# Pairwise flips of K and Q, and an own unit order for each segment of a group, in a two-branch attention kernel

## The chip, the cores and the metric

The kernel runs on one core of a Trainium2 chip. The metric is device time in microseconds (us) from the start to the end of one execution; a smaller one is better. A profiled execution gives the trace that all durations below come from.

The engines carry the names of the profile: PE multiplies matrices (PEld is its loading of the stationary operand), DVE is the vector engine, ACT the scalar engine (exponentials, logarithms, copies with a scale), POOL the general one, SP issues the DMAs. PE writes to PSUM, eight banks of 128 partitions by 512 fp32 words; DVE and ACT read PSUM and copy to SBUF.

## What is computed

A gate `g = sigmoid((x * gate_w).sum(-1))` mixes two branches on the same `x` (2048 tokens, 512 wide): `g * a + (1 - g) * b`.

Branch A is recurrent, segment by segment, 32 heads of 128:

```python
mem = mem0                                   # 8 rows
for s in range(64):                          # segments of 32 tokens
    h = concatenate([mem, x[32*s : 32*s+32]])     # 40 rows
    q, k, v = h @ Wq, h @ Wk, h @ Wv              # per head
    p = softmax(where(mask, q @ k.T * scale, -1e9))   # 40 x 40 for each head
    o = (p @ v) over all heads @ Wo               # 40 x 512
    mem = o[:8]                              # what the next segment starts from
    outs.append(o[8:])
```

Branch B is causal attention of 32 heads of 16 in four blocks of 512 tokens, with a memory of the earlier blocks (`M += phi(k).T @ v`, `z += sum phi(k)`), mixed by `sigmoid(beta)` and followed by `@ wo`. Its blocks do not wait for each other's attention.

All data are bf16; sums are fp32 in PSUM.

## The kernel before

Each engine gets a list of operations in the order in which the Python code records them (`Prog.op`). An operation waits by semaphore for the last writer of what it reads and the last readers of what it writes. PSUM banks are handed out when an operation is recorded (`Banks.take`, `pair`, `give`): an operation that gets a bank waits until the copy out of it has been made that last used it. So the order of recording sets both each engine's queue and which bank follows which.

First come the loads, the transpose of x and B's projections (to about 81 us of the trace). Then `plan_a` goes through the 64 segments of A, four to a group. Of a segment's 40 rows, 32 go through PE together: the 8 rows of memory and 24 tokens. The last 8 tokens of each of four segments ("left" rows) form a block of 32 rows that is projected a group ahead (`left_units`, L875), and their output projection and fold come a group later (`ol_units`, L938).

Within a segment the work is cut into units, and `A_ORDER` (L828) lists in which order they are recorded, the same list for every segment. b is 0 or 1, one for each half of the heads:

- `Q0x Q0y`, and so with K and V: the projection of half the heads, each in two halves of the contraction (x: channels that need the first half of the new memory, y: the second). `proj`, matmuls at L867.
- `k0 q0 v0`: the copy of such a projection out of PSUM, L320 on ACT or L322 on DVE, as `A_ENG` says (L832).
- `TK0 TQ0`: the flip. Four 32-row blocks of heads lie side by side over the partitions, and a 32 x 32 block transpose on DVE (`flip`, L872) makes them 128 x 32 per head.
- `S0`: scores, mask first (L1054), then 16 heads (L1057) and the left keys (L1061). `X0` exponential on ACT (L1070), `M0` row sums by a matmul with ones (L1087), `L0` logarithm and exponential for the reciprocal on ACT (L1094, L1097), `N0` the normalising multiply on DVE (L1101), `n0` its left part on POOL (L1107).
- `PV0`: values times probabilities (L1117) and at once its left part (L1126), into two pairs of banks; `E0a E0b` copy them out.
- `W0a` ... `W1b`: output projection (L908). `H0 l0`: its bf16 high half (copy on ACT, L915) and low half (subtraction on DVE, L920); `F0 F1` fold four partial sums into the new memory and rows (L930), `hm0 hm1` copy the memory to the next segment's input (L1163), `ax` copies the other rows (L1169).

Between these stand units of other work that PE can do meanwhile. `bS` takes one of B's 160 score blocks (matmuls at L711, and, in the same unit, the exponential on ACT at L719 and the causal mask on POOL at L727), if fewer than two are ahead of their PV; `bP` does the PV of a block (L758); `bT` does what follows every fifth one: a chain of seven small DVE operations (L791 to L807) behind a matmul bN (L786), or a transpose (L818). `Fc` and `Ff` take the next filler: the left projections with their copy and flip, the left rows' output projection with its high and low halves, its fold, or a group's final mixing (L991, L1006). B's blocks are spread over the first 57 segments (`nseg_b`, L851).

Of the kernel before, what the change touches and what calls it, by code (L numbers as in the profile page):

```python
# [223 lines left out]
def build(nc, es, A_x, A_mem0, A_Wq, A_Wk, A_Wv, A_Wo, B_wq, B_wk, B_wv, B_wo, B_beta, gate_w, out, dbg=None):  # L224
    v = NS()
# [30 lines left out]
    def alloc(stack, *specs):  # L256
        for name, shape, dt, n in specs:
# [24 lines left out]
    alloc(esA, ("LN_sb", [128, 2, 512], BF16, 0), ("KTL", [128, H, SEG], BF16, 2), ("QTL", [128, H, SEG], BF16, 2),  # L282
          ("VL", [128, 2, 512], BF16, 2), ("xL", [128, C, SEG], BF16, 2), ("KN_sb", [128, 2, 512], BF16, 0), ("QN_sb", [128, 2, 512], BF16, 0),
          ("KT_sb", [128, H, SEG], BF16, 0), ("QT_sb", [128, H, L], BF16, 0), ("V_sb", [128, 2, 512], BF16, 0),
# [84 lines left out]
def plan_const(v):  # L369
# [14 lines left out]
    sel(ident[:], [[-1, 128]], ALU.not_equal, 1.0, 0, 1, ri, "ident1")  # L384
    rz = Rs("KTz")
# [257 lines left out]
class BAttn:  # L643
# [3 lines left out]
    def __init__(self, v):  # L647
        self.v = v
        self.n = 0
        self.late = []  # L650
        self.total = 16 * 2 * 5
        self.pv_n = 0
        self.blocks = {}
        self.loaded = set()
        self.obk = None
        self.jobs_done = 0
# [27 lines left out]
    def scores(self):  # L684
# [30 lines left out]
        if k == 4:  # L715
            self.load(job + 1, G, "k")
        pt = v.PT[n % 2]
# [110 lines left out]
A_ORDER = """  # L828
    Q1x Q1y K0x K0y Q0x Q0y k0 K1x K1y V0x q0 q1 V0y k1 TK0 TQ0 v0 S0 TQ1 bP X0 bS V1x TK1 V1y M0 L0 v1
    S1 N0 X1 Fc M1 L1 n0 n1 PV0 E0a E0b N1 Fc bP PV1 W0a E1b W0b E1a bT W1b W1a H0 H1 bP l0 l1 bS  # L830
    Ff F0 F1 hm0 hm1 Ff bS ax Ff""".split()
A_ENG = dict(K0="act", K1="act", Q0="act", Q1="dve", V0="act", V1="dve", KL0="act", KL1="act", QL0="act", QL1="act", VL0="act", VL1="act", OL="act", ax="dve", hm="dve", n="gp", E0a="dve", E0b="act", E1a="act", E1b="act", last=0)  # L832


def plan_a(v, nseg):
# [14 lines left out]
    ORDER, ENG = DEV.get("order") or A_ORDER, DEV.get("eng") or A_ENG  # L850
    n_b0, nseg_b = bat.n, DEV.get("nseg_b", 57)  # L851
    last_half = 0 if ORDER.index("E1a") > ORDER.index("E1b") else 1
# [19 lines left out]
    def flip(dst, src, reads, writes, name):  # L872
        P.op("dve", lambda d: d.transpose(dst, src), reads=reads, writes=writes, name=name)  # L873

    def left_units(g):  # L875
# [7 lines left out]
        for m, w_sb, wr, nat in (("K", Wk_sb, "Wk", LN_sb), ("Q", Wq_sb, "Wq", LN_sb), ("V", Wv_sb, "Wv", VL[par])):  # L883
            rn = ["LN%d" % b if m != "V" else "VL%d_%d" % (par, b) for b in range(2)]
            for b in range(2):
                def u(m=m, w_sb=w_sb, wr=wr, nat=nat, b=b, rn=rn):
                    bk = B.take()
                    proj(bk, lhs, w_sb, b, m != "V", [Rs("xL%d" % par), Rs(wr)], "%sL%d_%d" % (m, g, b))
                    evac(ENG["%sL%d" % (m, b)], nat[:, b, :], pb[bk], [bk], [Rs(rn[b])], "%sLev%d_%d" % (m, g, b))
                    B.give(bk)  # L890
                    if m != "V":
                        dst = (KTL if m == "K" else QTL)[par]
                        flip(dst[:, 16 * b:16 * (b + 1), :], nat[:, b, :].rearrange("p (n e) -> p n e", e=SEG), [Rs(rn[b])],
                             [Rs("%sTL%d_%d" % (m, par, b))], "%sLt%d_%d" % (m, g, b))
                units.append(("c", u))
# [17 lines left out]
    def part_hi(bks, hf, hi, res, name):  # L913
        c = slice(HD * hf, HD * (hf + 1))
        P.op("act", lambda a: a.activation(hi[:, c], pb[bks[hf]][:, 0:HD], ACT.Copy), reads=[rbank[bks[hf]]],  # L915
             writes=[Rs(res[0][hf])], name="%sh%d" % (name, hf))
# [21 lines left out]
    def ol_units(g):  # L938
# [5 lines left out]
        for b in range(2):  # L944
            def u(b=b):
# [4 lines left out]
                if b == 1:  # L950
                    for hf in range(2):
                        part_hi(st["bks"], hf, LN_sb[:, 0, :], o_res, "olev%d" % g)
                        part_lo(st["bks"], hf, LN_sb[:, 0, :], LN_sb[:, 1, :], o_res, "olev%d" % g)
            units.append(("c", u))

        def ut():
            bks = B.pair()
            for hf in range(2):
                fold(bks, hf, LN_sb[:, 0, :], LN_sb[:, 1, :], o_res, "olf%d" % g)
            dst = aT_st[par][:, :, :].rearrange("p (a c) (r t) -> p a c r t", a=2, t=SEG)[:, :, :, :, SEG - 8:SEG]  # L960
# [9 lines left out]
        units.append(("f", ut))  # L970
        return units

    def tail_units(g):
# [11 lines left out]
        def ub():  # L985
# [7 lines left out]
            P.op("pe", f_, reads=[Rs("oTg"), Rs("woB")], writes=[rbank[bb]], name="brow%d" % g)  # L993
            P.op("act", lambda a: a.activation(t1_sb[:, :], pb[bb], ACT.Copy, scale=omg_sb[:, g:g + 1]),
# [5 lines left out]
        def uf():  # L1000
# [7 lines left out]
            P.op("pe", f_atr, reads=rr + [Rs("ident")], writes=[rbank[bk]], name="atr%d" % g)  # L1008
# [282 lines left out]
```

## Time and profile before

| | |
|---|---|
| three runs | 1028.02, 1028.87, 1029.57 us; median 1028.87 |
| profiled execution | 1029.02 us |
| span of its trace | 1027.3 us |
| granted share of PE's clock in it | 0.982 |
| PE, ACT, DVE, POOL busy | 91%, 64%, 57%, 25% of the span |
| first pass of A over the left rows | 81.96 us from the start |
| first and last copy of a new memory | 109.3 and 1018.7 us |

A row of a timeline has start, length, engine, line, operation, what is written and read, the shape, and a count of merged instructions; in brackets the idle time of the engine just before and what ended it. A row of groups has, behind the count, the total busy time, the mean of one in ns, and the idle time before. PE overlaps matmuls: a row of 16 that is 1.05 long may be followed by the next start after 0.87. What work costs PE is therefore read from one start to the next.

### The profile page before, as it was taken

How to read it: one execution, taken by the hardware profiler on the slowest of the kernel's cores; microseconds unless marked ns; L12 is line 12 of the kernel's file. 1: busy time of each engine (PE TensorE's matmuls, PEld its weight loads, DVE VectorE, ACT ScalarE, POOL GpSimd, SP SyncE). 2: the span in 40 equal slices, each digit the busy share in tenths (PEclk: the TensorE clock that was granted, in tenths of full speed). 3: DMA queues.
4: the chain of work that ended last, by engine and by line, in shares of the span. 5: the costliest groups of instructions: out<-in, count | busy, mean ns of one | idle time of the engine just before them, and what ended most of it. 6: DMA issues, size and time to landing. Idle time of an engine off the chain costs nothing. (4 is left out here: it accounts for less than half of the span.)

```text
span 1027.3 us, 57156 instructions
## 1 busy us (share of the span) xinstructions
PE 937.6 (91%) x25669; PEld 561.7 (55%) x25669; DVE 584.2 (57%) x1374; ACT 656.2 (64%) x1355; POOL 259.1 (25%) x672
## 2 busy tenths in 40 slices
PE   7986889999999999999999999999999999998886
PEld 4433555555555555555555555555555555555554
DVE  4673446555555656555556656555565556556553
ACT  3454577676676766676676666766676667765543
POOL 6201222222222222222222232222222222221110
PEclk9997899999999999999999999999999999999988
DMA  8897000000001111000001111010111001000010
GB/s 288 268 372 236 10 15 17 12 22 12 24 15 30 45 39 27 14 20 20 20 21 45 40 24 32 15 25 14 25 41 40 20 15 40 10 14 16 27 34 8
DMA packets 65900, 51.72 MB, mean 50 GB/s; under 512 B 34288, under 2 KB 64120, under 8 KB 64120
## 3 DMA queue, kind: packets, MB, share of 16 engines
q1 hardware_dynamic: 65656, 48.06, 16.0%
q8 instruction: 202, 3.31, 1.4%
q14 instruction: 42, 0.34, 0.1%
HBM read 33.47 MB, written 14.57 MB: 47 GB/s over the span
## 5 line engine op out<-in xcount | busy, mean ns | idle before, releaser
L727 POOL TENSOR_SCALAR_AFFINE_SELECT PT<-PT 128x256 bf16<-128x256 bf16 (+1 forms) x224 | 98.8, 441 | 387.5 <-ACT PT L719 345.8
L719 ACT ACTIVATE PT<-ps 128x1024 bf16<-128x1024 f32 x160 | 163.8, 1024 | 24.6 <-PE ps L711 12.0
L908 PE MATMUL ps<-Wo_sb,OT_sb 128*32 128x256 bf16 x4096 | 141.0, 282 | 13.2 <-DVE LN_sb L920 8.3
L867 PE MATMUL ps<-Wq_sb,hT 128*32 128x512 bf16 x2048 | 134.5, 382 | 2.2 <-ACT PT L719 1.3
L320 ACT ACTIVATE KN_sb<-ps 128x512 bf16<-128x512 f32 x128 | 76.5, 597 | 91.8 <-PE ps L867 86.5
L867 PE MATMUL ps<-Wk_sb,hT 128*32 128x512 bf16 x2048 | 133.8, 381 | 0.0
L867 PE MATMUL ps<-Wv_sb,hT 128*32 128x512 bf16 x2048 | 133.6, 380 | 0.0
L873 DVE STREAM_TRANSPOSE KT_sb<-KN_sb 128x512 bf16<-128x512 bf16 x128 | 88.4, 690 | 53.6 <-ACT KN_sb L320 53.6
L908 PEld LDWEIGHTS ps<-Wo_sb,OT_sb 128*32 128x32 bf16 x4096 | 101.8, 99 | 28.9 <-ACT OT_sb L320 11.9
L915 ACT ACTIVATE WH<-ps 128x256 bf16<-128x256 f32 x128 | 42.4, 381 | 91.5 <-PE ps L908 87.8
L873 DVE STREAM_TRANSPOSE QT_sb<-QN_sb 128x512 bf16<-128x512 bf16 x128 | 83.5, 690 | 10.0 <-ACT QN_sb L320 8.5
L920 DVE TENSOR_TENSOR WL<-ps,WH 128x256 bf16<-128x256 f32 x128 | 48.4, 419 | 67.5 <-ACT WH L915 32.8
L867 PEld LDWEIGHTS ps<-Wk_sb,hT 128*32 128x32 bf16 x2048 | 55.9, 97 | 55.5 <-DVE aTg L1009 1.9
L320 ACT ACTIVATE OT_sb<-ps 128x320 bf16<-128x320 f32 x192 | 76.0, 431 | 15.8 <-PE ps L1126 14.6
L867 PEld LDWEIGHTS ps<-Wq_sb,hT 128*32 128x32 bf16 x2048 | 50.0, 97 | 57.6 <-ACT PT L719 9.1
L1107 POOL TENSOR_TENSOR Pn_sb<-P_sb,R_sb 128x64 bf16<-128x64 bf16 x128 | 45.9, 359 | 137.5 <-ACT R_sb L1097 121.8
L322 DVE CAST V_sb<-ps 128x512 bf16<-128x512 f32 x64 | 44.3, 692 | 63.2 <-PE ps L867 63.2
L867 PEld LDWEIGHTS ps<-Wv_sb,hT 128*32 128x32 bf16 x2048 | 49.7, 96 | 53.5 <-issue 12.4
L322 DVE CAST QN_sb<-ps 128x512 bf16<-128x512 f32 x64 | 44.2, 691 | 43.1 <-PE ps L867 43.0
L711 PE MATMUL ps<-QTj,KTj 32*128 32x384 bf16 (+3 forms) x512 | 62.8, 302 | 3.8 <-ACT PT L719 2.2
L758 PEld LDWEIGHTS ps<-Vj,PT 128*128 128x128 bf16 x1280 | 42.6, 96 | 32.3 <-issue 31.1
L758 PE MATMUL ps<-Vj,PT 128*128 128x17 bf16 x1280 | 57.6, 172 | 0.0
(128 smaller groups left out, 1573.3 us busy)
## 6 DMA issues: line engine op xcount, KB each, us to landing
Wk_sb<-in_A_Wk_dram SPq DMA_DIRECT2D x4, 1024.0 KB, 7.2
Wq_sb<-in_A_Wq_dram SPq DMA_DIRECT2D x4, 1024.0 KB, 7.8
Wv_sb<-in_A_Wv_dram SPq DMA_DIRECT2D x4, 1024.0 KB, 9.5
Wo_sb<-in_A_Wo_dram SPq DMA_DIRECT2D x4, 1024.0 KB, 10.6
scr_vd<-V SPq DMA_DIRECT2D x16, 136.0 KB, 6.1
Vj<-scr_vd SPq DMA_DIRECT2D x32, 68.0 KB, 2.4
Wo_sb<-in_A_x_dram SPq DMA_DIRECT2D x4, 512.0 KB, 7.7
scr_kTd<-stgk SPq DMA_DIRECT2D x16, 128.0 KB, 6.5
```

The source lines that it names most:

```text
L320: P.op("act", lambda a: a.activation(dst, src, ACT.Copy), reads=[v.rbank[k] for k in bks], writes=dres, name=name)
L322: P.op("dve", lambda d: d.tensor_copy(dst, src), reads=[v.rbank[k] for k in bks], writes=dres, name=name)
L711: ins = pe.matmul(v.pb[bks[x]][:, o:o + w], KT[e][r, 128 * kc:128 * (kc + 1)], QT[r, q0:q0 + w], start=True, stop=True, tile_position=(r.s ...
L719: P.op("act", lambda a: a.activation(pt[:, :, :], v.ps[:, bks[0]:bks[1] + 1, :], ACT.Exp, scale=v.SCALE_B), reads=[v.rbank[b] for b in bks ...
L727: P.op("gp", lambda g, mv=mv: g.affine_select(mv, mv, [[0, mv.shape[1]], [1, 128]], ALU.is_ge, 0.0, base=0, channel_multiplier=-1), reads= ...
L758: ins = pe.matmul(v.pb[ob][:, o:o + 17], pt[:, x, col:col + 128], V[:, kc, 17 * h:17 * (h + 1)], start=first, stop=True, skip_group_check= ...
L867: ins = pe.matmul(pb[bk][SEG * j:SEG * (j + 1), :], lhs(c), cols(w, j) if split else w[:, 512 * j:512 * (j + 1)], start=(c == 0), stop=(c ...
L873: P.op("dve", lambda d: d.transpose(dst, src), reads=reads, writes=writes, name=name)
L908: ins = pe.matmul(pb[bks[hf]][SEG * j:SEG * (j + 1), 0:HD], lhs(4 * k + j), Wo_sb[:, 4 * k + j, HD * hf:HD * (hf + 1)], start=(first and k ...
L915: P.op("act", lambda a: a.activation(hi[:, c], pb[bks[hf]][:, 0:HD], ACT.Copy), reads=[rbank[bks[hf]]], writes=[Rs(res[0][hf])], name="%sh ...
L920: P.op("dve", lambda d: d.tensor_tensor(lo[:, c], pb[bks[hf]][:, 0:HD], hi[:, c], ALU.subtract), reads=[rbank[bks[hf]], Rs(res[0][hf])], w ...
L1107: P.op(ENG["n"], lambda d: d.tensor_tensor(left(Pn_sb), left(P_sb), grp04(R_sb[:, b, :]), ALU.mult), reads=[Rs("P%d" % b), Rs("R%d" % b)], ...
```

## The change

Five things change.

1. **Flips on pairs.** The copies of K and Q (those of the left rows too) out of PSUM now write so that two heads lie interleaved: element 0 of head one, element 0 of head two, and so on (`paired`: innermost step of two elements). The flip then reads and writes the tile as fp32, 128 x 256 elements of four bytes where it had 128 x 512 of two. KT, QT, KTL and QTL have the shape [128, 16 pairs, positions, 2], and a head is read with a step of two elements (`head`). In the setup, `ident` is flipped so and flipped back, by two DVE operations.
2. **Units cut apart.** B's exponential is a unit of its own (`bE`), with up to three score blocks ahead of PV and at most one whose exponential is not yet recorded. PV and its left part are two units (`PV0`, `PL0`). A filler's copies (with flip, or high and low half, or final mixing) are recorded by a later `Fe`, at the latest when two are pending. `ax0` and `ax1` are two units, `oL` (POOL's copy of the left rows' output) one.
3. **Four orders.** `A_ORDER` has one list for each of the four segments of a group.
4. **Engines.** Q0's and V0's copies go from ACT to DVE, and of the left rows the copies of the first half of K and of V. H's engine can be set, and stays ACT.
5. Fillers outside the segments are recorded whole, as before (`whole`).

The number of matmuls and their sizes stay.

What the instruction streams show of it, for the second segment of a group. First PE, from its start to the sums, before (names: hT is the segment's input, Wq_sb and so on the weights, QTj and KTj, Vj and PT are B's):

```order
L867 MATMUL ps<-Wq_sb,hT 32x512 x16
L867 MATMUL ps<-Wk_sb,hT 32x512 x16
L867 MATMUL ps<-Wq_sb,hT 32x512 x16
L867 MATMUL ps<-Wk_sb,hT 32x512 x16
L867 MATMUL ps<-Wv_sb,hT 32x512 x16
L1054 MATMUL ps<-mneg,ident 32x224 x4
L1057 MATMUL ps<-QT_sb,KT_sb 32x40 x16
L1061 MATMUL ps<-QT_sb,KTL 32x16 x16
L758 MATMUL ps<-Vj,PT 128x17 x8
```

and now:

```order
L890 MATMUL ps<-Wq_sb,hT 32x512 x8
L890 MATMUL ps<-Wk_sb,hT 32x512 x8
L890 MATMUL ps<-Wq_sb,hT 32x512 x8
L890 MATMUL ps<-Wk_sb,hT 32x512 x16
L890 MATMUL ps<-Wv_sb,hT 32x512 x8
L890 MATMUL ps<-Wq_sb,hT 32x512 x16
L1104 MATMUL ps<-mneg,ident 32x224 x4
L1107 MATMUL ps<-QT_sb,KT_sb 32x40 x16
L1111 MATMUL ps<-QT_sb,KTL 32x16 x16
L890 MATMUL ps<-Wk_sb,hT 32x512 x8
L890 MATMUL ps<-Wv_sb,hT 32x512 x8
L1137 MATMUL ps<-P_sb,onesb 32x160 x4
```

Half passes are interleaved, and the first scores stand behind eight halves where they stood behind ten. Next DVE in the same segment, from Q's first copy on, before (KN_sb, QN_sb are the copies, LN_sb those of the left rows):

```order
L322 CAST QN_sb<-ps 128x512
L873 STREAM_TRANSPOSE KT_sb<-KN_sb 128x512
L873 STREAM_TRANSPOSE QT_sb<-QN_sb 128x16x32 x2
L873 STREAM_TRANSPOSE KT_sb<-KN_sb 128x512
L322 CAST V_sb<-ps 128x512
L1101 TENSOR_TENSOR Pn_sb<-P_sb,R_sb 128x4x40
L873 STREAM_TRANSPOSE QTL<-LN_sb 128x512
L322 CAST OT_sb<-ps 128x320
L1101 TENSOR_TENSOR Pn_sb<-P_sb,R_sb 128x4x40
```

and now:

```order
L322 CAST QN_sb<-ps 128x8x2x32
L902 STREAM_TRANSPOSE QT_sb<-QN_sb 128x8x32
L902 STREAM_TRANSPOSE KT_sb<-KN_sb 128x256
L322 CAST QN_sb<-ps 128x8x2x32
L902 STREAM_TRANSPOSE QT_sb<-QN_sb 128x8x32
L902 STREAM_TRANSPOSE KT_sb<-KN_sb 128x256
L1151 TENSOR_TENSOR Pn_sb<-P_sb,R_sb 128x4x40
L322 CAST V_sb<-ps 128x512 x2
L1151 TENSOR_TENSOR Pn_sb<-P_sb,R_sb 128x4x40
L322 CAST OT_sb<-ps 128x320
L902 STREAM_TRANSPOSE QTL<-LN_sb 128x256 x2
```

Two more copies stand in the queue, both flips of one half of the heads come before the other half, and the left flips stand behind the output's copy. Last ACT in the same segment, from the first exponential on, before (P_sb is A's exponential, PT is B's, R_sb the reciprocal, OT_sb the output's copy):

```order
L1070 ACTIVATE P_sb<-ps 128x224
L719 ACTIVATE PT<-ps 128x1024
L1094 ACTIVATE R_sb<-ps 128x160
L1097 ACTIVATE R_sb<-R_sb 128x160
L1070 ACTIVATE P_sb<-ps 128x224
L320 ACTIVATE LN_sb<-ps 128x512
L1094 ACTIVATE R_sb<-ps 128x160
L1097 ACTIVATE R_sb<-R_sb 128x160
L320 ACTIVATE OT_sb<-ps 128x320
```

and now:

```order
L1120 ACTIVATE P_sb<-ps 128x224
L320 ACTIVATE KN_sb<-ps 128x8x2x32
L1144 ACTIVATE R_sb<-ps 128x160
L1147 ACTIVATE R_sb<-R_sb 128x160
L1120 ACTIVATE P_sb<-ps 128x224
L730 ACTIVATE PT<-ps 128x1024
L1144 ACTIVATE R_sb<-ps 128x160
L1147 ACTIVATE R_sb<-R_sb 128x160
L320 ACTIVATE OT_sb<-ps 128x320
```

B's exponential moved from ahead of the first reciprocal to ahead of the second; the left rows' copy that stood there comes later.

The diff, cut to its core:

```diff
-    ... ("KTL", [128, H, SEG], BF16, 2), ("QTL", [128, H, SEG], BF16, 2),
+    ... ("KTL", [128, H // 2, SEG, 2], BF16, 2), ("QTL", [128, H // 2, SEG, 2], BF16, 2),
...
+    pairs = lambda t: t.bitcast(F32).rearrange("p (n e) -> p n e", e=32)
+    P.op("dve", lambda d: d.transpose(pairs(v.etmp[0][:, 0:128]), pairs(ident[:, :])), reads=[ri], writes=[re], name="identp0")
+    P.op("dve", lambda d: d.transpose(pairs(ident[:, :]), pairs(v.etmp[0][:, 0:128])), reads=[re], writes=[ri], name="identp1")
...
+        self.exps.append((n, k, bks, diag))
+
+    def expo(self):
+        n, k, bks, diag = self.exps.pop(0)
+        self.e_n = n + 1
...
-A_ENG = dict(K0="act", K1="act", Q0="act", Q1="dve", V0="act", V1="dve", KL0="act", KL1="act", QL0="act", QL1="act", VL0="act", VL1="act", ...
+A_ENG = dict(E0a="dve", E0b="act", E1a="act", E1b="act", H0="act", H1="act", K0="act", K1="act", KL0="dve", KL1="act", OL="act",
+             Q0="dve", Q1="dve", QL0="act", QL1="act", V0="dve", V1="dve", VL0="dve", VL1="act", ax="dve", hm="dve", n="gp")
...
-    def flip(dst, src, reads, writes, name):
-        P.op("dve", lambda d: d.transpose(dst, src), reads=reads, writes=writes, name=name)
+    def paired(nat):
+        return nat.rearrange("p (m e u) -> p m u e", u=2, e=SEG)
+
+    def flip(dst, nat, reads, writes, name):
+        to = dst.rearrange("p m t u -> p m (t u)").bitcast(F32)
+        src = nat.bitcast(F32).rearrange("p (m e) -> p m e", e=SEG)
+        P.op("dve", lambda d: d.transpose(to, src), reads=reads, writes=writes, name=name)
...
-            evac(eng, nat[:, b, :], pb[bk], [bk], [Rs("%sN%d" % (m, b))], "%sev%d_%d" % (m, s, b))
+            dst, src = nat[:, b, :], pb[bk]
+            if m != "V":
+                dst, src = paired(dst), src.rearrange("p (m u e) -> p m u e", u=2, e=SEG)
+            evac(eng, dst, src, [bk], [Rs("%sN%d" % (m, b))], "%sev%d_%d" % (m, s, b))
...
+        head = lambda t, h: t[:, h // 2, :, h % 2]
...
         def b_s():
-            if bat.n < target and bat.n - bat.pv_n < 2:
+            if bat.n < target and bat.n - bat.pv_n < 3 and not bat.exps:
                 bat.scores()
+        def b_e():
+            if bat.exps and bat.e_n - bat.pv_n < 2:
+                bat.expo()
...
         def take_fill(mode):
+            if len(pend) > 1:
+                return
...
-        for u in ORDER:
+        for u in ORDER[r]:
             units[u]()
```

One of the four lists, for the second segment of a group:

```python
"""
Q0x K0x bE Q0y K0y K1x q0 TQ0 V0x Q1x Q1y k0 TK0 q1 S0 K1y X0 V0y TQ1 M0 k1 bS TK1 L0 bP V1x n0 S1 V1y X1 M1 Fc N0 bE v0 L1 v1 PV0 PL0
Fc N1 E0b bP E0a Fe n1 Fe PV1 PL1 W0a W0b E1b E1a bT W1b W1a H0 H1 l0 bS l1 Ff bP F0 Ff oL hm0 ax0 F1 hm1 bE ax1 Fe Fe"""
```

157 lines of the change are left out of this document (99 added, 58 removed).

## The prediction

> **What bounds the kernel now.** I read the page's busy times first, then PE's timeline over one segment, then the groups of instructions kept apart by form, then the timelines of ACT and DVE over the same segment, and last the waits of PE near the end.
>
> ```profile
> PE 937.6 (91%) x25669; PEld 561.7 (55%) x25669; DVE 584.2 (57%) x1374; ACT 656.2 (64%) x1355; POOL 259.1 (25%) x672
> ```
>
> PE is busy 91% of the span, but a busy PE includes matmuls that drain while nothing new starts. So I go by starts. This is PE over segment 29 (the second of its group). The columns are start, length, engine, line, and in brackets an idle time that the trace sees.
>
> ```profile
> 510.02 1.05 PE L867 MATMUL ps<-Wq_sb,hT 128*32 128x512 bf16 x16
> ...
> 514.34 0.27 PE L1054 MATMUL ps<-mneg,ident 128*32 128x224 bf16 x4
> ...
> 514.77 0.36 PE L758 MATMUL ps<-Vj,PT 128*128 128x17 bf16 x8
> 515.06 0.39 PE L711 MATMUL ps<-QTj,KTj 32*128 32x384 bf16 x4
> 515.38 1.05 PE L867 MATMUL ps<-Wv_sb,hT 128*32 128x512 bf16 x16
> 516.25 0.27 PE L1087 MATMUL ps<-P_sb,onesb 128*32 128x160 bf16 x8
> 516.35 0.27 PE L1054 MATMUL ps<-mneg,ident 128*32 128x224 bf16 x4
> ...
> 516.67 1.06 PE L867 MATMUL ps<-Wq_sb,xL 128*32 128x512 bf16 x16
> 517.55 0.28 PE L1087 MATMUL ps<-P_sb,onesb 128*32 128x160 bf16 x8
> 517.77 0.27 PE L1117 MATMUL ps<-Pn_sb,V_sb 32*128 32x40 bf16 x16
> ...
> 518.42 1.05 PE L867 MATMUL ps<-Wq_sb,xL 128*32 128x512 bf16 x16
> 519.40 0.36 PE L758 MATMUL ps<-Vj,PT 128*128 128x17 bf16 x8
> 519.86 0.28 PE L1117 MATMUL ps<-Pn_sb,V_sb 32*128 32x40 bf16 x16
> ...
> 520.15 1.06 PE L908 MATMUL ps<-Wo_sb,OT_sb 128*32 128x256 bf16 x32
> ...
> 522.36 0.36 PE L758 MATMUL ps<-Vj,PT 128*128 128x17 bf16 x8
> 522.65 0.39 PE L711 MATMUL ps<-QTj,KTj 32*128 32x384 bf16 x4
> 523.37 0.18 PE L930 MATMUL ps<-fold,WH 128*128 128x32 bf16 x1 [0.33 <-DVE WL L920]
> ...
> 523.70 0.18 PE L930 MATMUL ps<-fold,WH 128*128 128x32 bf16 x1
> ...
> 523.89 0.39 PE L711 MATMUL ps<-QTj,KTj 32*128 32x256 bf16 x4
> 524.22 0.62 PE L867 MATMUL ps<-Wq_sb,hT 128*32 128x512 bf16 x8
> ```
>
> The segment takes 524.22 - 510.02 = 14.20. What PE needs for it, where nothing waits: five passes in 4.32 and a sixth in 0.87, 5.19 together, 0.43 a half; scores S0 0.43; B's PV (bP) 0.29, three of them; B's scores (bS) 0.33, three; sums 0.10 (516.25 to 516.35), twice; S1 0.32 (to 516.67); two left projections of 0.88; PV with its left part 0.29, twice; the output projection with bN 2.21 (520.15 to 522.36); the folds 0.10 and 0.19. That is 5.19 + 0.43 + 0.87 + 0.99 + 0.20 + 0.32 + 1.76 + 0.58 + 2.21 + 0.29 = 12.84, so PE waits 1.36. Going down the rows, the waits are: 0.12 before PV0, 0.36 behind it, 0.10 and 0.17 before PV1, 0.39 before the first fold and 0.23 between the folds. All stand where A's own chain (K and Q copies, flips, scores, exponential, sums, reciprocal, PV, output, its low half, fold) is later than the work put beside it. So PE bounds the segment to nine tenths, and the chain the rest.
>
> **The change part by part.** Durations, by form (count, then busy us, mean ns):
>
> ```profile
> L873 DVE STREAM_TRANSPOSE KT_sb<-KN_sb 128x512 bf16<-128x512 bf16 x128 | 88.4, 690 | 53.6 <-ACT KN_sb L320 53.6
> L320 ACT ACTIVATE KN_sb<-ps 128x512 bf16<-128x512 f32 x128 | 76.5, 597 | 91.8 <-PE ps L867 86.5 <-DVE QN_sb L322 5.3
> L320 ACT ACTIVATE OT_sb<-ps 128x320 bf16<-128x320 f32 x192 | 76.0, 431 | 15.8 <-PE ps L1126 14.6
> L1070 ACT ACTIVATE P_sb<-ps 128x224 bf16<-128x224 f32 x128 | 44.2, 345 | 0.0
> L322 DVE CAST QN_sb<-ps 128x512 bf16<-128x512 f32 x64 | 44.2, 691 | 43.1 <-PE ps L867 43.0
> L1097 ACT ACTIVATE R_sb<-R_sb 128x160 f32<-128x160 f32 x128 | 43.1, 337 | 4.1
> L1101 DVE TENSOR_TENSOR Pn_sb<-P_sb,R_sb 128x160 bf16<-128x160 bf16 x128 | 43.0, 336 | 8.9 <-ACT R_sb L1097 0.4
> L1094 ACT ACTIVATE R_sb<-ps 128x160 f32<-128x160 f32 x128 | 38.7, 302 | 12.7 <-PE ps L1087 11.9
> L322 DVE CAST OT_sb<-ps 128x320 bf16<-128x320 f32 x64 | 30.3, 474 | 35.0 <-PE ps L1126 31.9 <-PE ps L908 3.2
> ```
>
> *Flips.* A flip now moves 256 four-byte elements for 512 two-byte ones. No row has a four-byte flip. From the casts of 512 and 320 elements DVE pays (691 - 474) / 192 = 1.13 ns an element, so 256 fewer save 0.29: 0.40. If it goes by bytes it stays 0.69. I take 0.40, since the row for 512 elements equals the cast of 512 elements, which goes by elements. Four flips a segment and four more a group on the left rows: 5 x 0.29 = 1.45 less on DVE a segment, and 0.29 less on the chain for each head half.
>
> *Engines.* Q0's and V0's copies go from ACT (597) to DVE (691), and of the left rows two copies in four segments. ACT sheds 2.5 x 0.60 = 1.5 a segment; DVE takes 2.5 x 0.69 = 1.73 and sheds 1.45, so 0.28 more. ACT was the fuller one (64% against 57%), so the two come level.
>
> *Writes and reads in steps of two.* The copies of K and Q write every second element, and PE reads KT, QT and KTL so. No row has this. Bounds for the copies: nothing, or twice the time per element, which is (597 - 431) / 192 = 0.86 ns on ACT, so 0.44 a copy, and 0.58 on DVE. I take nothing, as the nearest row, the copy of 512 to a dense tile, has the same count and source; the upper end is a rival below. [...] For PE's reads the upper end is the score matmuls taking twice their 0.32, so 0.64 x 64 = 41. I take nothing:
>
> ```profile
> L1061 PE MATMUL ps<-QT_sb,KTL 128*32 128x16 bf16 x2048 | 37.4, 171 | 0.0
> L1057 PE MATMUL ps<-QT_sb,KT_sb 128*32 128x40 bf16 x2048 | 34.5, 180 | 0.0
> ```
>
> The 2048 matmuls with 16 columns keep PE as long as the 2048 with 40, so how fast columns are read does not set them.
>
> *The two flips of ident* are 0.8 at most, on DVE in the load stage; taken as nothing, since even in the open they would not move the sum.
>
> *The order.* Here I walk PE through the new order for the second segment of a group, from Q0x at 0, with the unit costs above. Lags and B's exponential, on ACT, then the chain of bN and the low halves on DVE:
>
> ```profile
> 512.04 0.60 ACT L320 ACTIVATE KN_sb<-ps 128x512 bf16<-128x512 f32 x1 [0.90 <-PE ps L867]
> ...
> 515.55 1.02 ACT L719 ACTIVATE PT<-ps 128x1024 bf16<-128x1024 f32 x1
> ```
> ```profile
> 512.67 0.71 DVE L873 STREAM_TRANSPOSE KT_sb<-KN_sb 128x512 bf16<-128x512 bf16 x1 [0.86 <-ACT KN_sb L320]
> ...
> 520.84 0.22 DVE L791 RECIPROCAL rden<-ps 128x16 f32<-128x16 f32 x1
> ...
> 522.47 0.42 DVE L807 TENSOR_TENSOR amem<-ps,rden 128x256 f32<-128x256 f32 x1
> 522.81 0.74 DVE L920 TENSOR_TENSOR WL<-ps,WH 128x256 bf16<-128x256 f32 x2
> ```
>
> A pass is followed by its copy after 0.29 (the second pass ends at 510.02 + 2 x 0.865 = 511.75, the copy starts at 512.04), a copy by its flip after 0.03. Eight halves take PE to 3.46. K0's copy runs 2.02 to 2.62, Q0's on DVE 1.59 to 2.28, the flips end at 3.1: S0 finds its operands ready with 0.3 to spare, at 3.46 where it stood at 4.32. Then K1y, V0y, sums, bS, bP, V1x: 5.79. K1's copy is 4.50 to 5.10, its flip done at 5.5, so S1 starts at 5.79 (before: 516.35 - 510.02 = 6.33, with 516.25 + 0.10) and V1y ends at 6.54. The exponential of S1 ends at 6.75: **0.2** of waiting. Sums, then a left projection, to 7.73. On ACT a B exponential of 1.02 stands between that exponential and the logarithm of the second sums, so the reciprocal is done at 8.3; PV0, the other left projection and bP fill PE to 9.2; the normalising multiply and the copy of PV0 on DVE (0.34 + 0.47) end at 9.2, so PV1 waits **0.1**. Output with bN: 9.6 to 11.8. On DVE bN's chain of seven takes 520.84 to 522.89 = 2.05, behind the left flips, and ends at 12.35; only then come the low halves, 0.4 each, and the first fold at 12.85. bS and bP fill PE to 12.44: **0.4**, and **0.25** between the folds. In all 0.95 against 1.36.
>
> The three other orders walked the same way: the first leaves 0.75 (0.2 where the second K-left projection waits for a bank that the logarithm frees, 0.55 at the fold, bN's chain again), the third 0.8 (0.7 before PV1, which waits for the normalising multiply), the fourth 0.35. Together 2.85 a group against 4 x 1.36 = 5.44, 0.65 a segment. B's work lasts 57 segments: 57 x 0.65 = **37**.
>
> The last seven segments have no B work to fill with. One of them, from its output projection to its fold:
>
> ```profile
> 1000.18 3.34 PE L908 MATMUL ps<-Wo_sb,OT_sb 128*32 128x256 bf16 x64
> ...
> 1004.40 0.18 PE L930 MATMUL ps<-fold,WH 128*128 128x32 bf16 x1 [0.89 <-DVE WL L920]
> ```
>
> That is 4.22. In the segment above, the projection took 2.21 with bN in it, and the fold came 522.36 to 523.37 = 1.01 later: 3.2. The extra 1.0 is the projection's operands, whose copies on ACT come one by one behind the other work there; the new order puts them behind less. The scores are ready 0.3 earlier besides, of which I count 0.2: 7 x 1.2 = **8**.
>
> Sum: 45. The profiled execution took 1029.02 (span 1027.3 and 1.7 around it), the median is 1028.87, 0.15 less; 1028.87 - 45 = **984**.
>
> **The rivals.**
> - *The new orders fill more than my walk sees* (0.17). Successive copies on ACT overlap a little, which I left out; if a segment keeps 0.3 of waiting, 57 x 1.06 + 7 x 1.5 = 71: 958. For it: four orders instead of one. Against: bN's chain of 2.05 on DVE cannot shrink.
> - *The waits come back on DVE* (0.17). DVE gets 0.28 more a segment, and behind Q1's copy wait the flips, the V copies and the normalising multiply that PV1 needs. If V1's copy holds the multiply up by one copy less its slack, 0.4 a segment of the 0.65 returns: 1028.87 - 57 x 0.25 - 8 = 1007. [...]
> - *Slower: writes in steps of two cost* (0.11). At double time per element the copies of one K and one Q, 0.44 and 0.58, lie on the chain of both head halves, of which only the first has cover (0.3): 0.5 + 0.5 a segment x 64 = 64 against 45, about 1048. It decides from 0.35 a copy on, twice a segment (45 / 128). The dense-tile rows say nothing against it.
> - *The flip goes by bytes* (inside the second): 0.58 of chain a segment stays, at most 57 x 0.58 = 33 of the 45: 1017 at the far end.
>
> **How the numbers follow.** My forecast, 970 to 1000, has 0.52; the fuller gain 0.17; the smaller one, 1000 to 1026, 0.17; no change 0.03; slower 0.11. A measurement of this kernel tells about 0.2% (2 us) from no change. Faster 0.86, within 0.03, slower 0.11. For 8 in 10 the range reaches over most of the fuller and most of the smaller gain: 958 to 1013; outside stay the slower case and the ends.
>
> **What would show it.** Flips of 0.40, not 0.69; copies of K and Q at 0.60 and 0.69 as before; the score groups' starts 0.1 apart as before; mean segment in mid-kernel shorter by 0.65; in the second segment the fold still waiting for WL behind bN's chain; the last seven segments with the fold some 3.2 behind the start of the projection. Wrong if K's copy is longer than 0.8, if the flip is 0.69, or if PE's waits before PV1 have grown past 1.0 a segment.

## The result, and the profile after

The changed kernel takes 996.85 us (median of 4 runs, 996.13 to 1000.31), the kernel before 1028.76: a ratio of 0.970, 95% interval 0.967 to 0.972. That is 32 us gained where 45 was forecast. The profiled execution took 996.13, with a span of 994.1.

The page's row of busy times, after:

```profile
PE 925.5 (93%) x25669; PEld 546.3 (55%) x25669; DVE 619.1 (62%) x1536; ACT 579.9 (58%) x1195; POOL 259.8 (26%) x672
```

ACT sheds 76 us and DVE takes 35 more, and the two have changed places: DVE is now the fuller one. PE does the same work, in a shorter span.

The groups of instructions, kept apart by form, after (count, then busy us, mean ns):

```profile
L320 ACT ACTIVATE KN_sb<-ps 128x512 bf16<-128x512 f32 x128 | 96.9, 757 | 101.3 <-PE ps L890 100.2 <-DVE QN_sb L322 1.1
L322 DVE CAST QN_sb<-ps 128x512 bf16<-128x512 f32 x128 | 96.1, 751 | 62.5 <-PE ps L890 61.4
L322 DVE CAST V_sb<-ps 128x512 bf16<-128x512 f32 x128 | 87.1, 680 | 11.0 <-PE ps L890 10.2
...
L902 DVE STREAM_TRANSPOSE KT_sb<-KN_sb 128x256 f32<-128x256 f32 x128 | 57.0, 446 | 65.5 <-ACT KN_sb L320 64.5
...
L1107 PE MATMUL ps<-QT_sb,KT_sb 128*32 128x40 bf16 x2048 | 34.5, 181 | 0.0
```

The flip went from 690 ns to 446 with the same bytes and half the elements, so its time is not set by the bytes. The copies in steps of two were not free: K's on ACT went from 597 to 757, Q's on DVE from 691 to 751, while V's dense copy on DVE took 680 (692 before). PE's matmuls, which now read KT and QT in steps of two, did not move (180 before, 181 now).

To see where the time went, I count segments by the copies of the memory rows (`hT<-ps` on DVE), two a segment. A window from the first copy of one segment (the fourth) to the first copy of another, 53 segments on, holds 107 of them; the last seven segments, counted the same way, hold 15. Before, the row of each window (times of the first and last copy behind the colon):

```profile
L322 DVE CAST hT<-ps x107: 173/175/176, 150.5 to 921.3; 128x16 bf16<-128x16 f32 x107
...
L322 DVE CAST hT<-ps x15: 174/175/176, 921.3 to 1018.4; 128x16 bf16<-128x16 f32 x15
```

After:

```profile
L322 DVE CAST hT<-ps x107: 174/175/176, 145.8 to 893.0; 128x16 bf16<-128x16 f32 x107
...
L322 DVE CAST hT<-ps x15: 165/175/176, 893.0 to 985.1; 128x16 bf16<-128x16 f32 x15
```

A segment in mid-kernel went from 770.8 / 53 = 14.54 to 747.2 / 53 = 14.10, so **0.44** less (forecast 0.65), 23.6 in all. The last seven went from 97.1 to 92.1, **5.0** less (forecast 8). The remaining 4.7 of the profiled difference lies ahead of the first window. Of these, 1.8 lie behind the first copy of a new memory (109.3 before, 106.4 after, so 41.2 against 39.4 for three segments): more of the same gain. The other 2.9 lie in the stretch with the loads, where PE's granted clock is not the same (0.97 before and 1.00 after in the first 50 us). In mid-kernel it agrees to 0.01 (0.99 or 1.00 in every stretch of 250 from 150 to 900, in both traces). It is the third number from the end, before:

```profile
150.00:400.00 250.00, 236.27 (x6882) 143.27 (x6882) 145.31 (x342) 173.93 (x355) 64.80 (x164) 1.00 0.10 24
```

After:

```profile
150.00:400.00 250.00, 239.66 (x7084) 143.37 (x7080) 156.81 (x392) 155.97 (x322) 66.47 (x167) 1.00 0.10 24
```

Both run at 1.00 there, so segments compare cleanly; ahead of it the clock differs from execution to execution (0.93 to 1.00 in the first 50 us, 0.83 to 0.89 from 50 to 110, in seven traces), and over all that were profiled here the first window began anywhere from 145.8 to 154.6. I count nothing of the 2.9 as the change's.

PE over segment 29, the second of its group, after; the walk in the prediction starts at its Q0x, here 497.81:

```profile
497.81 0.61 PE L890 MATMUL ps<-Wq_sb,hT 128*32 128x512 bf16 x8
...
501.27 0.27 PE L1104 MATMUL ps<-mneg,ident 128*32 128x224 bf16 x4
...
503.74 0.27 PE L1104 MATMUL ps<-mneg,ident 128*32 128x224 bf16 x4
...
504.06 0.63 PE L890 MATMUL ps<-Wv_sb,hT 128*32 128x512 bf16 x8
504.82 0.28 PE L1137 MATMUL ps<-P_sb,onesb 128*32 128x160 bf16 x8
...
507.76 1.24 PE L943 MATMUL ps<-Wo_sb,OT_sb 128*32 128x256 bf16 x32
...
510.14 0.39 PE L716 MATMUL ps<-QTj,KTj 32*128 32x512 bf16 x2
...
511.09 0.18 PE L964 MATMUL ps<-fold,WH 128*128 128x32 bf16 x1 [0.27 <-DVE WL L954]
...
511.92 0.40 PE L890 MATMUL ps<-Wq_sb,hT 128*32 128x512 bf16 x4
```

S0 stands at 3.46, where the walk put it; S1 at 5.93 (walk: 5.79); the second sums at 7.01 (6.75), 0.76 behind a half pass of 0.43 and so after 0.33 of waiting (0.2); the projection at 9.95 (9.6), lasting 2.38 where 2.21 was counted; the fold at 13.28 (12.85). The next segment starts at 14.11. Each step slipped a little. The first slip is not a wait that the trace sees: from the first sums to the next start PE takes 0.22 where 0.10 was counted, and that is 0.12 of the 0.14 by which S1 is late.

So this segment took 14.20 before and 14.11 after: 0.09 gained, where the walk had 0.41. That is no accident of one segment. From the first Q pass of a segment to that of the next, averaged over the 13 groups from segment 4 to 55 (us):

| place in the group | before | after | gained | walked |
|---|---|---|---|---|
| first | 14.39 | 14.21 | 0.18 | 0.61 |
| second | 14.27 | 14.33 | -0.06 | 0.41 |
| third | 14.14 | 13.64 | 0.50 | 0.56 |
| fourth | 15.41 | 14.20 | 1.21 | 1.01 |

The walk had measured the waits of a second segment, 1.36, and taken them for all four. The fourth was over 1 us longer than the others, and two thirds of the gain were made there. About 0.25 of its 1.21 is work moved elsewhere: it has one PV of B (0.29) less in most groups, 2.0 a segment for 2.85. For the rest, two of PE's waits before (us in total, times, longest) stood in fourth segments, or in the last seven, alone: the output projection for the low half of the left rows (LN_sb), and PV behind the logarithm.

```profile
PE ps L908 <- DVE LN_sb L920: 8.3, 16, 0.8
...
PE ps L1117 <- ACT R_sb L1094: 6.2, 15, 0.4
```

After:

```profile
PE ps L943 <- DVE LN_sb L954: 0.7, 2, 0.5
```

The second of them is 0.8 in 2 times after.

### The profile page after: what moved, and what is told of

Its sections match the earlier page's. It is cut to its first block, busy times and chain, and to the rows that moved or that the text cites. A ratio compares the mean times of both kernels' runs of the same rounds, so it can differ in the third digit from the quotient of the medians.

```text
span 994.1 us, 57017 instructions
## 1 busy us (share of the span) xinstructions
PE 925.5 (93%) x25669; PEld 546.3 (55%) x25669; DVE 619.1 (62%) x1536; ACT 579.9 (58%) x1195; POOL 259.8 (26%) x672
## 4 chain that ended last, share of the span: by engine, by line
PE 81%; ACT 6%; DVE 5%; DMA 3%; issue 3%; SPq 0%; ACTq 0%; POOL 0%; DVEq 0%; POOLq 0%
PE ps L890 40%; PE ps L943 14%; PE ps L716 4%; PE ps L769 3%; PE ps L964 3%; PE ps L591 2%; PE ps L1167 2%; PE ps L1111 2%; PE ps L1137 2%; PE ps L566 2%; DMA scr_pQd<-stgp 2%; PE ps L1104 1%; PE ps L1031 1%; DMA Wo_sb<-in_A_Wo_dram 1%; PE ps L1107 1%
## 5 line engine op out<-in xcount | busy, mean ns | idle before, releaser
L320 ACT ACTIVATE KN_sb<-ps 128x512 bf16<-128x512 f32 x128 | 96.9, 757 | 101.3 <-PE ps L890 100.2
L890 PE MATMUL ps<-Wv_sb,hT 128*32 128x512 bf16 x2048 | 147.5, 380 | 0.3 <-ACT KN_sb L320 0.3
L890 PE MATMUL ps<-Wk_sb,hT 128*32 128x512 bf16 x2048 | 146.2, 382 | 0.1
L890 PE MATMUL ps<-Wq_sb,hT 128*32 128x512 bf16 x2048 | 142.2, 382 | 0.0
L322 DVE CAST QN_sb<-ps 128x512 bf16<-128x512 f32 x128 | 96.1, 751 | 62.5 <-PE ps L890 61.4
L902 DVE STREAM_TRANSPOSE KT_sb<-KN_sb 128x256 f32<-128x256 f32 x128 | 57.0, 446 | 65.5 <-ACT KN_sb L320 64.5
L322 DVE CAST V_sb<-ps 128x512 bf16<-128x512 f32 x128 | 87.1, 680 | 11.0 <-PE ps L890 10.2
L1120 ACT ACTIVATE P_sb<-ps 128x224 bf16<-128x224 f32 x128 | 45.7, 357 | 76.5 <-PE ps L1111 64.7
L890 PEld LDWEIGHTS ps<-Wk_sb,hT 128*32 128x32 bf16 x2048 | 50.6, 96 | 43.3 <-ACT KN_sb L320 1.5
L320 ACT ACTIVATE LN_sb<-ps 128x512 bf16<-128x512 f32 (+1 forms) x80 | 46.2, 604 | 35.1 <-PE ps L890 18.7
```

Of the source, the lines that this page charges most:

```text
L320: P.op("act", lambda a: a.activation(dst, src, ACT.Copy), reads=[v.rbank[k] for k in bks], writes=dres, name=name)
L322: P.op("dve", lambda d: d.tensor_copy(dst, src), reads=[v.rbank[k] for k in bks], writes=dres, name=name)
L890: ins = pe.matmul(pb[bk][SEG * j:SEG * (j + 1), :], lhs(c), cols(w, j) if split else w[:, 512 * j:512 * (j + 1)], start=(c == 0), stop=(c ...
L902: P.op("dve", lambda d: d.transpose(to, src), reads=reads, writes=writes, name=name)
L1120: P.op("act", lambda a: a.activation(P_sb[:, b, :], pb[bk][:, 0:224], ACT.Exp, scale=SCALE), reads=[rbank[bk]], writes=[Rs("P%d" % b)], na ...
```

## The experiments

My theory after the result: the new lists and engines carry the gain; the writes in steps of two, which I had priced at nothing, take part of it back. Rivals: the short flips carry it; the pairs are worth nothing; the orders themselves gave less than I walked. The experiments do not part the new lists from the cutting of units (point 2 of the change), which they need. The ratios below are to the kernel before on the same chip.

**Orders without pairs.** The flips go back to 2-byte elements, and the copies to dense writes:

```
-        to = dst.rearrange("p m t u -> p m (t u)").bitcast(F32)
-        src = nat.bitcast(F32).rearrange("p (m e) -> p m e", e=SEG)
-        P.op("dve", lambda d: d.transpose(to, src), ...)
+        src = nat.rearrange("p (n e) -> p n e", e=SEG)
+        P.op("dve", lambda d: d.transpose(dst, src), ...)
```

> The changed kernel with the flips of K and Q back on 2-byte elements and their copies dense again; orders, units and engines stay new. Flips should read 0.69 again, copies of K on ACT 0.60. My theory (the new orders carry most of the gain; a pair flip saves 0.245 on DVE, but its strided copy takes 0.16 of it back on ACT and 0.06 on DVE): 999 to 1005 us, a few us above the change. Rival 1 (the pairs carry the gain, order and units little): 1020 or more. Rival 2 (the pairs are worth nothing or cost): 997 or less.

Measured 1000.3 us, ratio 0.974 (0.970 to 0.978). So four fifths and more of the gain come without pairs. The first rival, that the pairs carry it, is out. The second, that they are worth nothing, is not settled by the time alone, since the interval touches the changed kernel's (0.967 to 0.972). The profile speaks against it by a little: 14.16 a segment in mid-kernel against 14.10, and 95.2 in the last seven against 92.1.

**Pairs without orders.** The same edit the other way round, in the kernel before.

> The kernel before with only the flips on 4-byte pairs: one list, the old engines, copies of K and Q in steps of two, flips of 0.445. My theory: the chain of a head half gets shorter by 0.085 where K sets it and 0.185 where Q does, so 1018 to 1026 us. Rival 1 (the pairs carry the gain): 1000 or less. Rival 2 (the pairs are worth nothing or cost): 1028 or more.

Measured 1026.9 us, ratio 1.0015 (0.999 to 1.004): nothing, at the edge of the second rival, and less gain than I had expected. One of its groups, by form:

```profile
L320 ACT ACTIVATE KN_sb<-ps 128x512 bf16<-128x512 f32 x128 | 98.4, 769 | 79.4 <-PE ps L867 71.1 <-DVE QN_sb L322 1.9
```

K's copy is as long as in the changed kernel and a little longer, on the engine that was the fuller one there.

**Copies without the step.** The changed kernel, writing densely without interleaving:

```
-                dst, src = paired(dst), src.rearrange("p (m u e) -> p m u e", u=2, e=SEG)
+                dst, src = dst.rearrange("p (m u e) -> p m u e", ...), src.rearrange("p (m u e) -> p m u e", ...)
```

> The changed kernel with copies of K and Q that write densely, while the flips stay on 4-byte words: the two heads of a pair are not interleaved, so the scores are not those of the reference; every count and every size stays. It measures the price of the writes in steps of two by itself. If the step costs the copy its time: K's copy on ACT 0.60 (0.757 in the change), Q's on DVE 0.69 (0.751). My theory (this price is what made the gain smaller than forecast, since it lies on A's chain): 983 to 990 us. Rival (the price is covered; the walk of the orders itself promised too much): 994 to 998, though the copies get shorter.

Measured 989.6 us, ratio 0.963 (0.960 to 0.967), within my range.

**The step on the other side.** The same interleaving, but in the order of the destination, so that SBUF is written densely and PSUM is read in steps of 32 elements:

```
-                dst, src = paired(dst), src.rearrange("p (m u e) -> p m u e", u=2, e=SEG)
+                dst, src = dst.rearrange("p (m e u) -> p m e u", u=2, e=SEG), src.rearrange("p (m u e) -> p m e u", u=2, e=SEG)
```

> The changed kernel with the same interleaving done from the other side: the copy goes through its elements in the order of its destination, so SBUF is written densely and PSUM is read in steps of 32 elements. The result is the same. If only the write in steps costs: copies of 0.60 on ACT and 0.69 on DVE, and a time like that of the dense copies, 983 to 990 by my theory. Rival (a step costs on either side, or costs more on PSUM's): copies of 0.75 or more, 996 or slower.

Measured 989.1 us, ratio 0.963 (0.959 to 0.967); its groups, by form:

```profile
L322 DVE CAST QN_sb<-ps 128x512 bf16<-128x512 f32 x128 | 88.4, 691 | 71.7 <-PE ps L890 71.7
...
L320 ACT ACTIVATE KN_sb<-ps 128x512 bf16<-128x512 f32 x128 | 76.4, 597 | 100.0 <-PE ps L890 96.3 <-DVE QT_sb L902 2.5 <-DVE QN_sb L322 1.1
```

The copies are back at 597 and 691 to the nanosecond: here the step costs where it is written (757 and 751), not where it is read. And this kernel, with the whole computation in it, is the fastest version here that keeps the change's lists. The same kernel was run a second time beside later ones:

> The kernel that reads PSUM in steps, again, beside the next two on the same chip. 0.963 of the kernel before.

Measured 989.9 us, ratio 0.965 (0.961 to 0.968). The changed kernel was run again as well:

> The changed kernel itself, beside the others on the same chip, for direct ratios. 0.97 of the kernel before.

Measured 995.4 us, ratio 0.969 (0.965 to 0.972). The intervals of single runs of the two kernels touch; but three runs with dense writes gave 0.963, 0.963 and 0.965, two with the step 0.969 and 0.970, and the traces agree. Of the second run of the kernel that reads in steps, the same two windows:

```profile
L322 DVE CAST hT<-ps x107: 173/175/177, 151.3 to 890.6; 128x16 bf16<-128x16 f32 x107
...
L322 DVE CAST hT<-ps x15: 166/175/176, 890.6 to 982.2; 128x16 bf16<-128x16 f32 x15
```

739.3 / 53 = 13.95 a segment (13.90 in the first run) against 14.10 and 14.07 in the two profiles of the changed kernel: 0.12 to 0.20 a segment is the price of the step. Against the 14.54 before, 0.59 to 0.64 is gained: in total nearly the walk's 0.65, though not where the walk had it. By place in the group, the second run gains 0.46, 0.00, 0.57 and 1.41.

**Short flips with dense copies in the old order.** The last edit in the kernel before.

> The kernel before with flips on 4-byte pairs and copies that write densely (reading PSUM in steps): flips of 0.445 for 0.690 and nothing paid for it, under the one old list. My theory (under the old list the flips have cover, since ten half passes stand ahead of the first scores, so a shorter chain to the scores is worth nothing there): 1022 to 1028, within 0.5% of before. Rival (the shorter flips pay by themselves, 0.49 a segment): 1000 or less.

Measured 1022.9 us, ratio 0.994 (0.992 to 0.997). So the short flips are worth 0.6% in the old order, a little more than nothing and than the 0.5% I had allowed, and the step ate all of it there (1.0015). In the new order they are worth 0.010 without the step (0.974 to 0.964); with it, about half of that, which is not clear of the intervals.

**The old engines under the new lists.** Four entries of the table go back (the text below says five, and names four).

```
-A_ENG = dict(..., KL0="dve", ..., Q0="dve", ..., V0="dve", ..., VL0="dve", ...)
+A_ENG = dict(..., KL0="act", ..., Q0="act", ..., V0="act", ..., VL0="act", ...)
```

> The changed kernel with the engines of before for five copies: Q0, V0 and the left rows' K0 and V0 back on ACT (Q0 and K0 of a segment then follow each other on one engine). The orders stay. My theory (the gain lies in the orders, and they need Q0's copy beside K0's): ACT gets 1.5 us a segment back and Q0's flip comes 0.75 later, of which 0.3 had cover, so 0.3 to 0.5 a segment: 1015 to 1030. Rival (the engines matter little, the order alone carries it): 1000 or less.

Measured 1039.2 us, ratio 1.012 (1.008 to 1.016): slower than before the change, by more than I had expected. The direction is my theory's, and part of the loss stands where it looked. In the third segment of a group, number 30, PE, then ACT, then DVE:

```profile
539.64 0.60 PE L890 MATMUL ps<-Wk_sb,hT 128*32 128x512 bf16 x8
540.91 0.28 PE L1104 MATMUL ps<-mneg,ident 128*32 128x224 bf16 x4 [0.67 <-ACT PT L730]
```
```profile
538.63 0.78 ACT L320 ACTIVATE KN_sb<-ps 128x512 bf16<-128x512 f32 x1 [2.49 <-PE ps L890]
539.24 0.77 ACT L320 ACTIVATE QN_sb<-ps 128x512 bf16<-128x512 f32 x1
```
```profile
540.04 0.45 DVE L902 STREAM_TRANSPOSE QT_sb<-QN_sb 128x256 f32<-128x256 f32 x1 [3.36 <-ACT QN_sb L320]
540.41 0.40 DVE L902 STREAM_TRANSPOSE KT_sb<-KN_sb 128x256 f32<-128x256 f32 x1
```

Both copies run on ACT one behind the other, the list then flips Q ahead of K, and K's flip ends at 540.81, 0.10 before the scores. The row of PE puts the wait down to B's exponential (PT), which also stands behind the two copies on ACT and ends at 540.87. Segment 60, the first of its group, tells the two apart: it lies behind B's work and has no exponential of B. PE, then DVE:

```profile
986.72 0.28 PE L1104 MATMUL ps<-mneg,ident 128*32 128x224 bf16 x4 [0.60 <-issue]
```
```profile
986.22 0.40 DVE L902 STREAM_TRANSPOSE KT_sb<-KN_sb 128x256 f32<-128x256 f32 x1
```

PE waits 0.60, as in the first segments that have the exponential, and K's flip again ends 0.10 before the scores, so the flip alone accounts for the wait. In the first and third segments of a group PE waits 0.60 and 0.67: 19.0 us in the 30 places that carry PT's name. Another 7.9 in 29 places is PV0 waiting for V's copy, which is back on ACT too. The rest of the 44 us was not traced.

**The new engines under the old list.** The same four moves, in the kernel before, with 2-byte flips.

> The kernel before with only the engine table's four moves that its list knows: the copies of Q0, V0 and of the left rows' K0 and V0 on DVE for ACT; 2-byte flips, one list, no split units. My theory (lists and engines were fitted to each other: the new lists with the old engines lost 44 us): alone they give little or lose, 1020 to 1045, since in the old list V0, the flips and Q0 then queue on DVE ahead of the first scores while 2-byte flips still take 0.69. Rival (ACT was the engine that held the chain, relieving it is the gain): 1005 or less.

Measured 1094.2 us, ratio 1.066 (1.062 to 1.071): 68 us lost, more than three times the worst I had allowed (1045). Its waits of PE (us in total, times, longest), and DVE ahead of one of those scores, which start at 544.40:

```profile
PE ps L1054 <- DVE QT_sb L873: 56.4, 64, 0.9
```
```profile
541.85 1.29 DVE L322 CAST QN_sb<-ps 128x512 bf16<-128x512 f32 x2 [2.59 <-PE ps L867]
543.05 0.70 DVE L873 STREAM_TRANSPOSE KT_sb<-KN_sb 128x512 bf16<-128x512 bf16 x1
543.68 0.67 DVE L873 STREAM_TRANSPOSE QT_sb<-QN_sb 128x512 bf16<-128x512 bf16 x1
```

Both copies of Q and both flips run on DVE without a gap, 2.5 us in a row, and the first scores wait in each of the 64 segments. Lists and engines are one change: either alone loses (the lists were tried alone with the pairs, the engines without), and both together gain 2.6% even without pairs. Which of the four copies does the harm was not tried one by one.

**B's chain behind the fold.** In the kernel that reads in steps, the unit that sends bN and its chain on DVE moves, in all four lists; the second one:

```
-... W0a W0b E1b E1a bT W1b W1a H0 ... F1 hm1 bE ax1 Fe Fe
+... W0a W0b E1b E1a W1b W1a H0 ... F1 hm1 bE ax1 bT Fe Fe
```

> The kernel that reads PSUM in steps, with the unit that sends B's normalising chain moved in all four lists from before the output projection's last quarter to behind the last copy out of the fold's banks. My theory (the fold's wait for the low halves, 11 us in 25 times, stands behind that chain of 2.05 us on DVE, and there the chain has room beside the next segment's passes): 6 to 10 us less than that kernel, ratio to before 0.954 to 0.958. Rival (the chain then delays Q's copy and its flip at the head of the next segment, and the first scores wait instead): 0.963 or more.

Measured 1020.7 us, ratio 0.993 (0.991 to 0.996), so some 30 us lost against the 0.963 of that kernel. Its waits of PE:

```profile
PE ps L890 <- DVE amem L818: 18.7, 19, 1.4
PE ps L964 <- DVE WL L954: 11.0, 25, 0.9
```

My theory falls, twice. The fold's waits for the low halves are what they were: 11.0 in 25 times, and 11.4 in 25 where the chain stood ahead of it. The chain was not their cause. The changed kernel's own profile says so too: the chain runs in 32 of the 64 segments (in eight of them shorter), and 15 of its 25 waits of this kind lie in the others, as in segment 41:

```profile
682.77 0.18 PE L964 MATMUL ps<-fold,WH 128*128 128x32 bf16 x1 [0.27 <-DVE WL L954]
```

The rival's time came true, but not by its mechanism, Q's copy: the price was a bank. PE in one such place:

```profile
518.28 1.05 PE L890 MATMUL ps<-Wq_sb,hT 128*32 128x512 bf16 x16
520.26 1.05 PE L890 MATMUL ps<-Wk_sb,hT 128*32 128x512 bf16 x16 [0.94 <-DVE amem L818]
```

K's pass reads nothing that the chain writes, so what it waits for is a bank: the chain's banks of PSUM come free with its last step, the one that writes amem. Here that step runs from 519.79 to 520.21, and K's pass starts 0.05 behind it. These waits are 18.7 of the some 30 us; the rest was not traced.

**The second sums behind other work.** In the kernel that reads in steps, PE waits 0.32 for the exponential ahead of the second sums, in the second and the fourth segment of every group. First the second list, then the fourth as well:

```
-... S1 V1y X1 M1 Fc N0 bE ...
+... S1 V1y X1 Fc M1 N0 bE ...
-... X1 v1 M1 PV0 PL0 ...
+... X1 v1 PV0 M1 PL0 ...
```

> The same kernel with the second sums (M1) behind the next left projection in the second segment's list, where PE waits 0.32 for the exponential of the second scores in each of the 16 segments; B's exponential holds ACT there anyway until the sums would be needed. My theory (the walk's wait at M1 has free cover next to it): 16 x 0.2 to 0.32, 3 to 5 us less, ratio 0.958 to 0.960. Rival (the reciprocal comes later and PV1 waits instead): no less, 0.963 or more.

> As the run with the second segment's list changed, and in the fourth list the second sums behind PV0 as well, where PE waits 0.32 too. My theory: another 2 to 5 us less, ratio 0.953 to 0.957, if PV0's operands (the normalising multiply, V0's copy) are ready 0.3 earlier. Rival (they are not: PV0 waits for them in the sums' place): no less than with the second list alone.

Measured 990.1 and 989.5 us, ratios 0.965 (0.961 to 0.968) and 0.964 (0.960 to 0.967), against 0.965 beside them: nothing. The wait did go. PE in segment 37, with the sums as they were:

```profile
612.44 0.61 PE L890 MATMUL ps<-Wq_sb,hT 128*32 128x512 bf16 x8
...
619.55 1.04 PE L890 MATMUL ps<-Wq_sb,xL 128*32 128x512 bf16 x16
...
623.62 1.06 PE L943 MATMUL ps<-Wo_sb,OT_sb 128*32 128x256 bf16 x32
```

and with the sums behind the left projection:

```profile
611.97 0.62 PE L890 MATMUL ps<-Wq_sb,hT 128*32 128x512 bf16 x8
...
618.66 1.05 PE L890 MATMUL ps<-Wq_sb,xL 128*32 128x512 bf16 x16
...
623.03 1.27 PE L943 MATMUL ps<-Wo_sb,OT_sb 128*32 128x256 bf16 x32
```

The left projection starts 6.69 after the segment's start instead of at 7.11, so 0.42 earlier. Of that 0.15 is left at PV0 (7.93 for 8.08), 0.12 at the second half of the output projection (11.06 for 11.18), and 0.03 at the end of the segment (13.93 for 13.96). In between ACT sets the place: from B's exponential on, it works almost without a pause through the logarithm, the reciprocal's exponential, a copy of PV0, two left copies, and only then the copies of PV1 that the projection needs. From 619.29 to 623.37 the trace marks one idle time of ACT, of 0.16, and from 618.83 to 622.79, with the sums moved, none. With the sums as they were, then with the sums moved:

```profile
622.60 0.77 ACT L320 ACTIVATE OT_sb<-ps 128x320 bf16<-128x320 f32 x2
```
```profile
622.02 0.77 ACT L320 ACTIVATE OT_sb<-ps 128x320 bf16<-128x320 f32 x2
```

These copies end at 623.37 and 622.79, and the projection's second half starts 0.25 and 0.24 behind them. In the fourth list it is the same: from the last half pass of V to the left rows' output projection, segment 39 takes 1.41 with the sums in either place. A wait of PE was closed, and the next one on the same chain opened.

## Why the prediction was right, and where its size was off

*The direction and the mechanism* held: the orders fill waits of PE, and the walk from the old trace's unit costs gave 0.65 a segment where the runs without the step show 0.59 to 0.64. That this total agrees so well is in part luck. The walk started from the 1.36 of waiting in a second segment and took it for all four places. In the second places nothing was gained (0.41 walked), and the fourth, which had more waiting than any other, made up for it (1.21 with the step and 1.41 without, 1.01 walked). None of the signs of being wrong came: K's copy took 0.757 (limit 0.8), the flip 0.446, and no wait of PE before a PV was longer than 0.9 (limit 1.0). The size was off by 13 us, in these terms:

- **"Writes and reads in steps of two … I take nothing"** is the step that failed. The copies cost 0.160 more on ACT and 0.060 on DVE, inside the bounds (0.44 and 0.58) but not at their lower end. The runs with and without it put it at about 0.5% of the time, 5 to 7 us; by segments, 0.12 to 0.20 x 57 = 7 to 11. The same mechanism was the slower rival, with a turning point at 0.35 a copy; it ran at half of that and less. Its share of PE's reads was nothing, as taken (score matmuls of 181 ns for 180).
- **The late segments, 7 x 1.2 = 8**, gave 5.0. I had read the 4.22 from projection to fold off segment 62 and taken it for all seven. In the trace before, only the last three stand at 4.2 to 4.3; the four ahead of them at 3.2 to 3.5. Segment 59:

```profile
957.69 0.40 PE L908 MATMUL ps<-Wo_sb,OT_sb 128*32 128x256 bf16 x8
...
961.09 0.18 PE L930 MATMUL ps<-fold,WH 128*128 128x32 bf16 x1 [0.52 <-DVE WL L920]
```

  That is 3.40. Segment 61, one of the last three, which took 4.28 before, gives 2.81 after:

```profile
957.18 1.93 PE L943 MATMUL ps<-Wo_sb,OT_sb 128*32 128x256 bf16 x64
959.99 0.18 PE L964 MATMUL ps<-fold,WH 128*128 128x32 bf16 x1
```

  Over the seven the mean went from 3.74 to 3.08, so 0.66 a segment, 4.6 in all, where I had counted 1.0 and 0.2 more for the scores.
- **The flips** cost 0.446, not 0.40: the price of an element read off two casts, 1.13 ns, was too high, and 690 less 446 over 256 elements gives 0.95, if an element costs the same in both. So each flip saves 0.245 and not 0.29, and with the step on K's copy the chain of a K half is 0.085 shorter.
- **The first fold's wait "behind bN's chain"** in the second segment was there, 0.27 for 0.4, but its cause was not: with the chain moved away it stayed, and segments without the chain have it too. The walk had that chain in the first and second segments of every group; it runs in 32 of the 64 segments. What remains in my reading is the low halves' own way from the projection through ACT and DVE, with too little filler beside it; that was not tried by itself. So the fuller gain that I held back "since bN's chain cannot shrink" was held back for a wrong reason.
- **Engines**, which I had costed as a balance of busy time (1.5 less on ACT, 0.28 more on DVE), were no balance: undone, they cost 44 us; done alone, 68. What counts is which copies stand side by side ahead of the first scores. This did not harm the sum, since the walk had placed them, but the rival built on it ("the waits come back on DVE") looked for the harm at V1's copy, where it did not come.

By segments, the 37 of mid-kernel came to 25 (0.44 x 57), 12 less, and the 8 of the late segments to 5, 3 less; the 2.9 of the stretch with the loads makes up for about 2 of these 15. Of the 12, the step is 7 to 11, or 5 to 7 by the medians. The 1 to 5 that are left by segments I did not take apart. Open, too, is how the gain divides between the four lists and the units cut apart for them.

## What to carry to other kernels

An order list and an engine table fitted together are one change: try neither alone, and price a copy's engine by what stands beside it ahead of the next consumer, not by busy totals. When a layout needs interleaving, put the step on the side that the trace shows to be free, here the read from PSUM (597 ns on ACT and 691 on DVE, as without a step; 757 and 751 with the step in the write). A wait that is visible on PE was worth nothing to close here, where the engine behind it, ACT, was itself busy but for 0.16 us in 4.1; look at its queue up to the next thing that PE needs from it. And read the waits in each place of a repeating pattern before multiplying one of them: here the place that was walked in detail gained nothing, and two thirds of the gain came from another.

## What the runs showed of the hardware

- A copy of 128x512 from PSUM that writes bf16 to every second element of SBUF took 757 ns for 597 on ACT and 751 for 691 on DVE (the changed kernel, and the kernel before).
- Reading PSUM in steps of 32 fp32 elements instead, with dense writes, took 597 and 691, as the plain copy; for these reads by ACT and DVE no price showed.
- A flip of K's 128x256 four-byte elements took 446 ns in the changed kernel, and one of 128x512 two-byte elements 690 in the kernel before. Both move the same bytes, so the time of these flips is not set by the bytes; if an element costs the same in both, it costs 0.95 ns. The flips of 128x64 four-byte elements in the setup took 245 and 246, which gives 1.05 an element among the four-byte ones.
- Score matmuls whose operands lie in steps of two bf16 took 181 ns, as with dense ones (180).
